# Four transformer blocks on one core: GpSimd takes part of the linear layer's products, z is read from PSUM, late score fills look for a free row group, and the build-time scheduler gets new issue times and a finer plan

## The chip, the core and the metric

The kernel runs on one core of a Trainium2 chip. The core has five engines that run their own instruction queues in order and wait for each other by semaphores: PE (TensorE, matmuls, with its weight loads shown apart as PEld), ACT (ScalarE), DVE (VectorE), POOL (GpSimd) and SP (SyncE, which only issues DMAs here). The metric is the device time of one execution in microseconds (us).

## What is computed

The input x has 2048 tokens of 512 values. Four blocks follow each other, each added to x after a layer norm: A, B, A, B, with the same weights in both A and both B.

```python
def _A_ref(x, wq, wk, wv, wo):            # 32 heads of 16, one K and V for all heads
    q = (x @ wq).reshape(B, S, H, Dh).transpose(0, 2, 1, 3)
    k, v = x @ wk, x @ wv
    p = softmax(einsum("bhqd,bkd->bhqk", q, k) * Dh ** -0.5)
    return einsum("bhqk,bkd->bhqd", p, v).transpose(0, 2, 1, 3).reshape(B, S, H * Dh) @ wo

def _B_ref(x, wqkv, wo):                  # linear attention, 32 heads of 16
    q, k, v = split(x @ wqkv)
    phi = lambda t: where(t > 0, t + 1, exp(t)) + 1e-6
    pq, pk = phi(q), phi(k)
    kv = einsum("bhsd,bhse->bhde", pk, v)
    z = einsum("bhsd->bhd", pk)
    num = einsum("bhqd,bhde->bhqe", pq, kv)
    den = einsum("bhqd,bhd->bhq", pq, z)[..., None] + 1e-6
    return (num / den).transpose(0, 2, 1, 3).reshape(B, S, D) @ wo

x = x + _A_ref(layernorm(x), ...)
x = x + _B_ref(layernorm(x), ...)
x = x + _A_ref(layernorm(x), ...)
x = x + _B_ref(layernorm(x), ...)
```

An A block and the B block after it are called a layer here, so there are two layers.

## The kernel before

**Who sets the order.** The order of the instructions isn't written out by hand. When the kernel is built, `Sched` runs a small model of the core: each operation is given to `add` with the engines that may do it, an estimated duration for each, what it reads and writes, a priority, and the buffers it takes and frees. Whenever an engine is free in the model, the ready operation with the smallest priority goes onto its queue. The result is five fixed queues, with semaphore waits where one operation needs another of a different engine (`finalize`, `emit`). So a change of the model's durations moves instructions on the chip. The model's knobs (priorities such as `PZ` and `PX`, limits such as `LEAD`, `DMIN` and `NPX`) are global names, and `PLAN` sets them anew at given model times, every 12 us.

**Attention (A).** The scores of one head, one key tile and 512 queries (in the first and last quarter: four heads of 128 queries) are a piece: 128 by 512, one bank of PSUM. There are 2048 pieces in a layer, 4096 in all. A piece's score matmul (L884) uses one row group of PE, 32 of the 128 rows, and up to four pieces on different row groups run beside each other. The exponentials are shared by two engines:

- ACT takes three banks or two at a time (`fill`): one exp (L1041) over 1536 or 1024 columns of PSUM into PTA.
- DVE takes single pieces from further on in the list, the late fills (`dstep`): L1098, called P1, makes an approximate exponential by integer arithmetic into PTD; three shifted copies of it are made for four pieces at once on DVE (L1169, called xo) or piece by piece on POOL (L1159, called xp), and the sum with four weighted copies of V corrects the approximation.

The products with V (L921, `pv`) add into bank 7 from both: one matmul for a piece of ACT, four for a piece of DVE. `norm` then copies the sums out (Eo, L933), transposes, divides and passes them on to the output projection, whose result is added to x (L1273).

**The B block.** While attention still runs, `b_prep` takes each finished token tile: layer norm, projections, and phi, which is an exp on ACT (L1281), a maximum on DVE (L1288, phr), a minimum on POOL (L1290, phm) and a sum on POOL (L1292, phs). `kv_block` sums k^T v and z over groups of tiles in PSUM; `kvm` (L1363) multiplies the result by a mask into kvacc or kvtmp, and kva (L1366) adds kvtmp to kvacc. At the last group zf (L1370) and kvf (L1372) add the two, zf is spread to zb (L1378), and den, the B block's denominators, can start.

From there each of the 16 token tiles goes through `b_tile`: den on PE; ln and exp(-ln) on ACT (L1409, L1410), which give 1/den; pqn on DVE (L1411), which multiplies pq by it; y2 on PE (num and output projection in one); and the residual (L1426 on DVE, or L1427 as a copy on DVE or ACT when PE has added x itself). After the first layer each tile goes straight into the second layer's layer norm (L692, L693, L695, L696, xn L711), its transposition (L723, xnT L729) and its K, V and Q (Kr L754/L755, Vaug L775, QT L808), so the layers overlap in a handover. After the second layer each tile is written out by a DMA.

**Rules of the model that matter here.** An operation with `port=True` on DVE isn't started while POOL works, and POOL isn't started while such an operation runs on DVE. A piecewise shift on POOL (`pair`) is made to wait for the DVE instruction before the last one planned, so that on the chip POOL doesn't run ahead of the plan. `idle` adds dummy matmuls where PE would be too quiet.

Of the kernel before, what the change touches and what calls it, by code (L numbers as in the profile page):

```python
# [11 lines left out]
ALU = mybir.AluOpType  # L12
# [8 lines left out]
LX = 0.338  # L21
# [32 lines left out]
PQL = 3.988  # L54
NPX = 6
# [5 lines left out]
SWITCH, PASS = 0.1, 0.217  # L61
PLAN = (
    (0.0, {'LX': 0.338, 'HOLD': 0.836, 'LEAD': 17, 'LEAD2': 14, 'NT0': 3, 'DMIN': 2, 'MP': 1, 'AP': 0.771, 'MF': 0.758, 'AF': 3.03, 'PCONT': 0.992, 'PX': 0.523, 'EVP': 1.5, 'EVX': 1.016, 'PQP': 3.044, 'PB': 1.6, 'PY': 4.497, 'PKV': 4.5, 'PTR': 1.57, 'PQL': 3.988, 'PHL': 3.959, 'PZ': 0.317, 'BK': 2.611, 'BKX': 0.376, 'BKR': 0.5, 'NPX': 6, 'PXP': 1.839, 'PXM': 0.451, 'PXA': 4.0}),
    (12.0, {'DMIN': 0, 'PX': 0.9, 'PXP': 2.685}),
    (24.0, {'LEAD': 16, 'DMIN': 1, 'AF': 2.905, 'PX': 0.523, 'PHL': 2.067, 'PZ': 0.131, 'PXP': 1.839, 'PXM': 0.53}),
    (36.0, {'LEAD2': 15, 'AF': 3.184, 'EVP': 1.614, 'PHL': 3.855, 'BKX': 0.07, 'PXM': 0.55}),
    (48.0, {'LEAD2': 14, 'AF': 2.533, 'PCONT': 0.746, 'PX': 1.328, 'EVP': 1.5, 'EVX': 1.127, 'PHL': 3.586, 'BKX': 0.376, 'NPX': 5}),
    (60.0, {'HOLD': 0.734, 'EVP': 0.64, 'PB': 3.033, 'PY': 3.776, 'PHL': 3.273, 'BKX': 0.628}),
    (72.0, {'AP': 0.2, 'PX': 2.292, 'PQP': 1.722, 'PB': 4.5, 'PXP': 1.517, 'PXM': 0.551}),
    (84.0, {'NT0': 5, 'PCONT': 0.778, 'EVX': 1.857}),  # L70
    (96.0, {'AF': 2.605, 'PHL': 1.421, 'BKR': 0.006}),
    (108.0, {'HOLD': 0.836, 'NT0': 3, 'AP': 0.771, 'AF': 2.905, 'PCONT': 0.78, 'PX': 3.908, 'EVP': 1.5, 'EVX': 1.016, 'PQP': 3.892, 'PB': 1.6, 'PY': 4.497, 'PQL': 2.469, 'PHL': 3.855, 'PZ': 0.906, 'BKX': 0.376, 'BKR': 0.5, 'NPX': 6, 'PXP': 1.839, 'PXM': 0.532}),
    (120.0, {'LX': 0.248}),
    (132.0, {'LX': 0.338, 'HOLD': 0.88}),
    (144.0, {'HOLD': 0.836, 'AP': 0.818, 'MF': 0.966, 'AF': 2.533, 'PCONT': 0.746, 'PX': 1.328, 'EVX': 1.127, 'PQP': 3.044, 'PQL': 3.988, 'PHL': 3.586, 'PZ': 0.131, 'NPX': 5, 'PXM': 0.55}),
    (156.0, {'AP': 0.771, 'MF': 0.758, 'AF': 2.905, 'PCONT': 0.992, 'PX': 3.679, 'EVX': 1.016, 'PY': 3.528, 'PQL': 3.445, 'PHL': 2.801, 'PZ': 1.146, 'BKR': 0.395, 'NPX': 6}),
    (168.0, {'HOLD': 0.57, 'NT0': 5, 'AP': 0.2, 'AF': 2.605, 'PCONT': 0.778, 'PX': 2.292, 'EVP': 0.64, 'EVX': 1.994, 'PQP': 1.6, 'PB': 4.5, 'PY': 3.776, 'PKV': 1.749, 'PQL': 3.988, 'PHL': 1.421, 'PZ': 0.131, 'BKX': 0.628, 'BKR': 0.006, 'NPX': 5, 'PXP': 1.517, 'PXM': 0.551}),
    (180.0, {'LEAD2': 24, 'PXM': 0.248}),
    (192.0, {'LX': 0.248, 'HOLD': 0.836, 'LEAD2': 14, 'NT0': 3, 'AP': 0.771, 'AF': 2.905, 'PCONT': 0.78, 'PX': 3.908, 'EVP': 1.5, 'EVX': 1.016, 'PQP': 3.892, 'PB': 1.6, 'PY': 4.497, 'PKV': 4.5, 'PQL': 2.469, 'PHL': 3.855, 'PZ': 0.906, 'BKX': 0.376, 'BKR': 0.5, 'NPX': 6, 'PXP': 3.89, 'PXM': 0.532}),
    (204.0, {'EVX': 2.046, 'PKV': 3.197, 'PXP': 4, 'PXM': 0.284}),  # L80
    (216.0, {'LX': 0.426, 'MF': 0.635, 'PQL': 1.0, 'BK': 2.24}),
    (228.0, {'HOLD': 0.674, 'EVX': 2.017, 'PB': 1.741, 'PKV': 3.92, 'PHL': 2.483, 'PXA': 3.668}),
    (240.0, {'HOLD': 0.655, 'BKR': 0.693}),
    (252.0, {'LX': 0.248, 'HOLD': 0.836, 'MF': 0.134, 'PX': 3.309, 'EVX': 2.046, 'PB': 1.6, 'PKV': 3.197, 'PQL': 2.469, 'PHL': 3.035, 'BK': 2.611, 'BKR': 0.637, 'PXA': 4.0}),
    (264.0, {'MF': 0.758, 'PX': 3.908, 'EVP': 2.13, 'PHL': 3.855, 'BKX': 1.267, 'BKR': 0.5, 'NPX': 5}),
    (276.0, {'DMIN': 2, 'EVP': 1.033}),
    (288.0, {'LX': 0.255, 'PX': 3.59, 'PTR': 1.67, 'BKR': 0.556}),
    (300.0, {'HOLD': 0.688, 'MP': 2, 'PQP': 2.339, 'PZ': 0.624, 'PXM': 0.374, 'PXA': 3.256}),
    (312.0, {'HOLD': 0.698, 'PX': 3.335, 'EVP': 1.382, 'PKV': 1.911, 'NPX': 6, 'PXM': 0.475}),
    (324.0, {}),  # L90
    (336.0, {'HOLD': 0.836, 'LEAD2': 16, 'MP': 1, 'PX': 2.368, 'EVP': 1.033, 'PQP': 3.892, 'PKV': 3.197, 'PZ': 0.906, 'BKX': 0.72, 'NPX': 5, 'PXM': 0.284, 'PXA': 4.0}),
    (348.0, {'LX': 0.338, 'HOLD': 0.743, 'LEAD2': 14, 'DMIN': 1, 'PCONT': 0.992, 'PX': 0.523, 'EVP': 1.5, 'EVX': 1.016, 'PQP': 4.5, 'PY': 4.236, 'PKV': 4.5, 'PTR': 1.57, 'PQL': 3.988, 'PZ': 0.131, 'BKX': 0.376, 'BKR': 0.5, 'NPX': 6, 'PXP': 1.839, 'PXM': 0.55}),
    (360.0, {}),
    (372.0, {'LX': 0.009, 'MF': 0.59, 'PY': 4.5}),
    (384.0, {'LX': 0.338, 'HOLD': 0.836, 'MF': 0.758, 'PCONT': 1.275, 'PX': 1.223, 'EVP': 0.567, 'PQP': 4.254, 'PY': 4.497, 'PZ': 0.225, 'PXA': 4.921}),
# [1396 lines left out]
```

## Time and profile before

| what | us |
|---|---|
| median of 3 runs | 1521.6 (1520.04 to 1524.15) |
| the profiled execution | 1516.72 |
| its span, first to last instruction | 1515.0 |
| mean granted TensorE clock | 0.997 of full speed |

| stage (by the trace) | from, to |
|---|---|
| ramp: loads, first layer norms, K, V, Q, first exps | 0 to some 42 us |
| attention of layer 1, with most of its B block's preparation | to some 720 |
| handover: last sums of B, its 16 tiles, start of layer 2 | to some 791 |
| attention of layer 2 | to some 1470 |
| end: last sums of B, its 16 tiles, output | to 1515 |

The costliest groups by line are the exps on ACT (L1041, 1187 of them, 1365.5 us busy), P1 on DVE (L1098, 1121, 744.5 us), the shifts on POOL (L1159, 1076, 659.2 us) and on DVE (L1169, 574, 392.0 us). PE's matmuls overlap, so its groups don't sum to its busy time. The 32 products pqn (L1411) on DVE have a mean of 682 ns. DMA moves 18 MB and is busy for a few per cent of the span.

A row of the profile's groups gives line, engine, operation, output and input, number, busy time, mean ns of one, and the engine's idle time just before them with what ended it. Records of an engine overlap a little at their ends, so a mean can be longer than the distance between two starts.

### The profile page before, as it was taken

The page shows a single profiled execution, that of the slowest core. Times are in us where ns is not written, and L with a number is a line of the kernel's source. Part 1 is how long each engine was busy: PE and PEld are TensorE (multiplying, and loading weights), DVE is VectorE, ACT ScalarE, POOL GpSimd, SP SyncE. Part 2 cuts the span into 40 slices and gives each one's busy share as a digit, 9 for nine tenths or more (in the row PEclk, how much of TensorE's full clock was granted, in tenths as well). Part 3 has the DMA queues.
Part 4 walks back from the last instruction along what each step waited for, and adds up shares of the span by engine and source line. Part 5 has one row for each costly group of instructions (what it writes and reads, how often), then busy time and mean ns, then how long its engine had stood idle before and what let it go on. Part 6 is the DMA issues. An engine that isn't in the chain of part 4 may idle for free.

```text
span 1515.0 us, 42368 instructions
## 1 busy us (share of the span) xinstructions
PE 1465.7 (97%) x18389; PEld 494.5 (33%) x18392; DVE 1373.7 (91%) x2419; ACT 1458.6 (96%) x1443; POOL 814.5 (54%) x1293
## 2 busy tenths in 40 slices
PE   6999999999999999999799999999999999999997
PEld 4333233322333222333453232332333232233334
DVE  6899998999988999899799999989998799989987
ACT  6999999999999999999699999999999999999986
POOL 2455666655574655565325645565555644465551
PEclk9999999999999999999999999999999999999999
DMA  4000000000000000000000000000000000000001
GB/s 142 2 8 8 5 9 8 4 4 4 16 8 5 5 5 16 9 9 8 3 3 4 6 9 5 12 6 5 5 5 15 5 5 5 5 19 9 5 9 59
DMA packets 46187, 17.98 MB, mean 12 GB/s; under 512 B 39856, under 2 KB 45488, under 8 KB 46000
## 3 DMA queue, kind: packets, MB, share of 16 engines
q1 hardware_dynamic: 46000, 15.27, 4.2%
q8 instruction: 144, 2.36, 0.6%
q14 instruction: 43, 0.35, 0.1%
HBM read 5.28 MB, written 2.10 MB: 5 GB/s over the span
## 4 chain that ended last, share of the span: by engine, by line
PE 48%; ACT 44%; DVE 7%; issue 1%; DMA 0%
ACT PTA L1041 41%; PE ps_all L921 19%; PE ps_all L884 19%; PE ps_all L632 9%; DVE PTD L1098 2%; PE ps_all L942 1%; DVE PTD L1169 1%; ACT e_buf L1281 1%; DVE stats L692 1%; DVE xn_buf L711 1%; DVE e_buf L1288 1%; DVE pqT L1411 0%; ACT e_buf L1409 0%; DVE Eo L933 0%; ACT e_buf L1410 0%
## 5 line engine op out<-in xcount | busy, mean ns | idle before, releaser
L1041 ACT ACTIVATE PTA<-ps_all 128x1536 bf16<-128x1536 f32 (+1 forms) x1187 | 1365.5, 1293 | 12.1 <-PE ps_all L884 8.8
L1159 POOL TENSOR_SCALAR PTD<-PTD 128x512 uint16<-128x512 uint16 x1076 | 659.2, 621 | 558.0 <-DVE PTD L1169 414.4
L1098 DVE TENSOR_SCALAR PTD<-ps_all 128x512 uint16<-128x512 f32 x1121 | 744.5, 683 | 76.0 <-PE ps_all L884 67.9
L884 PE MATMUL ps_all<-QT,Kr 32*128 32x512 bf16 x4147 | 654.2, 384 | 13.4 <-ACT PTA L1041 7.0
L921 PE MATMUL ps_all<-PTD,Vaug 128*32 128x512 bf16 x4484 | 614.1, 384 | 4.8 <-DVE Eo L933 3.4
L921 PE MATMUL ps_all<-PTA,Vaug 128*32 128x512 bf16 x2975 | 525.8, 386 | 0.0
L1169 DVE TENSOR_SCALAR PTD<-PTD 128x2048 uint16<-128x2048 uint16 x574 | 392.0, 702 | 1.7
L884 PEld LDWEIGHTS ps_all<-QT,Kr 32*128 32x128 bf16 x4147 | 161.3, 91 | 485.1 <-ACT PTA L1041 229.7
L921 PEld LDWEIGHTS ps_all<-PTD,Vaug 128*32 128x32 bf16 x4484 | 158.0, 94 | 204.8 <-issue 134.2
L921 PEld LDWEIGHTS ps_all<-PTA,Vaug 128*32 128x32 bf16 x2975 | 131.2, 94 | 167.6 <-issue 134.1
L632 PE MATMUL ps_all<-wqkv_sb,xnT 128*32 128x512 bf16 x1024 | 78.8, 396 | 3.0 <-ACT xnT L729 1.4
L1281 ACT ACTIVATE e_buf<-ps_all 128x512 f32<-128x512 f32 x64 | 40.2, 632 | 15.6 <-PE ps_all L632 10.9
L779 POOL TENSOR_SCALAR Vaug<-Vaug 128x32 bf16<-128x32 bf16 x48 | 15.2, 318 | 73.5 <-ACT Vaug L775 38.9
L1288 DVE TENSOR_SCALAR e_buf<-ps_all 128x512 f32<-128x512 f32 x60 | 40.9, 684 | 12.2 <-ACT e_buf L1281 11.8
L1290 POOL TENSOR_SCALAR e_buf<-e_buf 128x512 f32<-128x512 f32 x60 | 38.1, 637 | 23.1 <-ACT e_buf L1281 22.4
L632 PE MATMUL ps_all<-xnT,wq_sb 128*32 128x128 bf16 (+1 forms) x896 | 41.8, 298 | 3.6 <-issue 3.5
L692 DVE BATCH_NORM_STATS2 stats<-x_sb 128x6 f32<-128x512 bf16 x64 | 42.9, 678 | 1.2 <-DMA x_sb<-in_A_x_dram 1.0
L933 DVE COPY Eo<-ps_all 128x512 f32<-128x512 f32 x63 | 42.9, 681 | 1.1 <-PE ps_all L921 0.8
L632 PE MATMUL ps_all<-wo_sb,OT 128*32 128x512 bf16 x512 | 43.4, 382 | 0.0
L1292 POOL TENSOR_TENSOR pqT<-e_buf 128x512 bf16<-128x512 f32 x30 | 41.2, 1376 | 3.4 <-DVE e_buf L1288 2.9
L942 PE MATMUL ps_all<-identf,Eo 128*128 128x128 f32 x256 | 42.0, 287 | 0.2 <-DVE e_buf L1288 0.2
L1292 POOL TENSOR_TENSOR pk_tok<-e_buf 128x512 bf16<-128x512 f32 x30 | 39.4, 1312 | 0.8 <-DVE e_buf L1288 0.5
(88 smaller groups left out, 672.1 us busy)
## 6 DMA issues: line engine op xcount, KB each, us to landing
out_dram<-x_sb SPq DMA_DIRECT2D x16, 128.0 KB, 2.2
OT<-Osb SPq DMA_TRANSPOSE x120, 2.4
xnT<-xn_buf SPq DMA_TRANSPOSE x120, 2.4
wqkv_sb<-in_B_wqkv_dram SPq DMA_DIRECT2D x1, 1536.0 KB, 11.7
x_sb<-in_A_x_dram SPq DMA_DIRECT2D x3, 256.0 KB, 3.1
x_sb<-in_A_x_dram SPq DMA_DIRECT2D x1, 768.0 KB, 7.7
wq_sb<-in_A_wq_dram SPq DMA_DIRECT2D x1, 512.0 KB, 5.6
x_sb<-in_A_x_dram SPq DMA_DIRECT2D x1, 512.0 KB, 8.6
```

The source lines that it names most:

```text
L632: i = e.matmul(out[32 * c:32 * c + 32], lhsT=lhsT[:, 32 * c:32 * c + 32], rhs=rhs, start=start, stop=stop, skip_group_check=True)
L692: add(DV, tdv(512), lambda e: e.bn_stats(stats[:, t, 0:6], x_sb[:, t, :]), reads=[("x", t)], writes=[("st", t)], prio=prio, name="bn")
L884: x = e.matmul(bank(b0 + k), lhsT=Kr[r, m, kt * P:(kt + 1) * P], rhs=QT[r, self.units[u][0] % 2, gs, q0:q0 + n], start=True, stop=True)
L921: return e.matmul(ps[32 * c:32 * c + 32, 7 * 512:8 * 512], lhsT=Vaug[:, kt, r, :], rhs=src() if callable(src) else src, start=opened[0], s ...
L942: i = e.transpose(bank(ht.idx, P, qs * P), Eo[:, he.idx, qs * P:(qs + 1) * P], identf[:])
L1041: oe = add(AC, tac(m * 512), lambda e: e.activation(PTA[:, hp.idx, 0:m * 512], bank(SETS[s][0], m * 512), ACTF.Exp, scale=SCALE), deps=[o] ...
L1098: o = add(DV, tdv(512), lambda e: e.tensor_scalar(out=PTD[:, hp.idx, i * 512:(i + 1) * 512], in0=bank(db), scalar1=SCALE * LOG2E * 128.0, ...
L1159: return e.tensor_scalar(out=PTD[:, ht.idx, i * 512:(i + 1) * 512], in0=PTD[:, hp.idx, i * 512:(i + 1) * 512], scalar1=float(SHIFT[r]), sc ...
L1169: return e.tensor_scalar(out=PTD[:, ht.idx, 0:512 * m], in0=PTD[:, hp.idx, 0:512 * m], scalar1=float(SHIFT[r]), op0=ALU.add, **kw)
L1281: o1 = add(AC, tac(512), lambda e: e.activation(e_buf[:, he.idx, :], bank(h.idx), ACTF.Exp), deps=[o], uses=[h], acq=[he] if fast else [he ...
L1288: o2 = add(DV, tdv(512), lambda e: e.tensor_scalar(out=e_buf[:, hr.idx, :], in0=bank(h.idx), scalar1=0.0, scalar2=1e-6, op0=ALU.max, op1=A ...
L1292: add(PO, PHS, lambda e: e.tensor_tensor(out=dst, in0=sh(e_buf[:, hr.idx, :]), in1=sh(e_buf[:, he.idx, :]), op=ALU.add), deps=[o2, o3], us ...
```

## The change

Five things change in the scheduler and the operations, and with them the plan.

1. **Issue times in the model.** After issuing a score fill PE is taken up for 0.0045 us and 0.011 more for each further row group (before: 0.004). A shift on POOL costs 0.035 us less. A result of DVE counts as seen by POOL 0.05 us later. Any POOL operation longer than 0.4 us, not only the piecewise shifts, now waits for the last DVE instruction planned, or the one before it when DVE is at work in the model.
2. **Late fills.** `dstep` also avoids row groups on which a score matmul is still running in the model, when PE's last work was a score fill.
3. **Products on POOL.** pqn may go to DVE or POOL.
4. **z from PSUM.** zf adds kvacc and the PSUM columns of z themselves, before kvm, instead of kvacc and kvtmp after it.
5. **The plan** has a step every 4 us instead of 12, with new values; `BASE` holds what is set first. A new knob `NZ` adds a small fixed pseudo-random amount to priorities over 0.9, with the seed `SD`.

`activity` is written in a shorter way with the same values.

```diff
+JF = 1
+NZ = 0.0
+SD = 0
+PQE = 1
+ZD = 1
...
-    (12.0, {'DMIN': 0, 'PX': 0.9, 'PXP': 2.685}),
...
+    (1040.0, {'MF': 0.877, 'EVP': 2.53, 'PXM': 0.488}),
+    (1044.0, {}),
+    (1048.0, {'HOLD': 0.88, 'EVX': 0.959, 'PHL': 3.249, 'PXM': 0.595, 'PXA': 4.935, 'SD': 257}),
...
-PHM, PHS, POW, PXO, PXN = 0.62, 1.27, 0.92, (0.1, 1.1e-3), 0.62
+PHM, PHS, POW, PXO, PXN = 0.62, 1.27, 0.92, (0.035, 1.1e-3), 0.62
...
+        self.nadd += 1
+        if NZ and prio > 0.9:
+            o.prio += NZ * ((self.nadd * 40503 + SD * 9973) % 1009 / 1009.0 - 0.5)
...
-        return d.vis
+        return d.vis + (0.05 if d.eng == DV and o.engs[0] == PO else 0.0)
...
-        if e == PO and o.pair and len(self.order[DV]) > 1:
-            o.deps = o.deps + [self.order[DV][-2]]
+        if e == PO and (o.pair or o.dur[PO] > 0.4) and len(self.order[DV]) > 1:
+            o.deps = o.deps + [self.order[DV][-2 if self.tfree[DV] > self.now + 1e-9 else -1]]
...
-        self.tfree[e] = end if e != PE or o.pk[0] == "F" else self.now + 0.004
+        self.tfree[e] = end if e != PE or o.pk[0] == "F" else self.now + 0.0045 + (0.011 * (len(o.pk[1]) - 1) if o.pk[0] == "S" else 0.0)
...
-        def dstep(self, db, js):
+        def dstep(self, db, jset):
+            js = set(jset)
...
+            if sc.pk == "S" and JF:
+                js |= {j for j in range(4) if sc.pgrp.get(j, 0.0) > sc.now}
             good = [j for j in range(4) if j not in used and j not in js] or [j for j in range(4) if j not in js] or range(4)
...
-            js.add(self.pos[p][2])
+            jset.add(self.pos[p][2])
...
+            if final and ZD:
+                gs = slice(2 * hh, 2 * hh + 2)
+                add(DV, 0.07, lambda e, hh=hh, gs=gs, h=h: e.tensor_tensor(out=zf[:, gs], in0=kvacc[:, hh, 2 * P:KW], in1=bank(h.idx, 2, 2 * P), op=ALU.add),
+                    reads=[("kva", hh)], deps=[o], uses=[h], writes=[("zf", hh)], prio=PZ - 0.02, name="zf")
...
-                add(DV, 0.07, lambda e, hh=hh, gs=gs: e.tensor_tensor(out=zf[:, gs], in0=kvacc[:, hh, 2 * P:KW], in1=kvtmp[:, hh, 2 * P:KW], op=ALU.add),
-                    reads=[("kvt", hh), ("kva", hh)], writes=[("zf", hh)], prio=PZ - 0.02, name="zf", port=True)
...
-        o = add(DV, tdv(512), lambda e: e.tensor_tensor(out=pqT[:, :, ts], in0=pqT[:, :, ts], in1=e_buf[:, he.idx, :].rearrange("p (g n) -> p g n", g=NG), op=ALU.mult),
+        o = add((DV, PO) if PQE else DV, {DV: tdv(512), PO: PHS}, lambda e: e.tensor_tensor(out=pqT[:, :, ts], in0=pqT[:, :, ts], in1=e_buf[:, he.idx, :].rearrange("p (g n) -> p g n", g=NG), op=ALU.mult),
...
-    globals().update(PLAN[0][1])
+    globals().update(BASE)
```

Since the scheduler decides, the diff alone doesn't tell what moves. In the built programs these counts differ:

| engine, operation | before | after |
|---|---|---|
| ACT exps of three banks | 603 | 599 |
| ACT exps of two banks | 582 | 582 |
| ACT exps of one bank | 2 | 0 |
| ACT copies xnT, QT, Eo, steps zb | 13, 6, 1, 6 | 14, 7, 2, 8 |
| ACT copies Kr, Vaug, Msb | 11, 4, 4 | 7, 2, 3 |
| DVE P1 | 1121 | 1135 |
| DVE products pqn | 32 | 12 |
| POOL products pqn (13 in the handover, 7 at the end) | 0 | 20 |
| POOL piecewise shifts | 1076 | 1120 |
| DVE Kr, Vaug, Msb, xnT, zb | 21, 12, 4, 21, 2 | 25, 14, 5, 20, 0 |
| PE products with V: of PTA, of PTD | 2975, 4484 | 2961, 4540 |
| PE score matmuls | 4147 | 4135 |
| PE dummy matmuls (32 columns wide) | 140 | 112 |

At the end the built order now has the two sums kva before the last residual of attention; before, they stood between the last layer norm's statistics and its xn.

## The prediction

> **What bounds the kernel now.** I read the page's engine line first, then busy time by stage, the chain that ended last, and the single rows that the change touches.
>
> ```profile
> PE 1465.7 (97%) x18389; PEld 494.5 (33%) x18392; DVE 1373.7 (91%) x2419; ACT 1458.6 (96%) x1443; POOL 814.5 (54%) x1293
> ```
>
> Two engines look full. Matmuls are pipelined, so PE's 97% is not PE at its peak; the chain of waits has ACT's line L1041 (the exp) as its largest item, 41% of the span. The busy time in five stretches shows where ACT is full and where it is not (columns: length, then busy us of PE, weight loads, DVE, ACT, POOL; then the granted clock):
>
> ```profile
> 60.00:690.00 630.00, 619.72 (x6915) 195.53 (x6910) 585.36 (x997) 624.75 (x564) 373.72 (x581) 1.00 0.04 8
> 744.00:789.00 45.00, 40.98 (x1214) 25.25 (x1208) 41.76 (x102) 43.59 (x97) 7.38 (x22) 1.00 0.02 4
> 795.00:1450.00 655.00, 647.84 (x7177) 202.78 (x7173) 606.12 (x1040) 649.43 (x585) 360.31 (x562) 1.00 0.04 7
> 1478.00:1490.80 12.80, 7.53 (x221) 4.10 (x218) 8.83 (x20) 5.83 (x14) 5.54 (x6) 0.87 0.00 1
> 1490.80:1508.40 17.60, 16.44 (x455) 8.79 (x447) 16.69 (x28) 17.38 (x35) 0.00 (x0) 1.00 0.26 86
> ```
>
> In both attention stretches ACT is busy over 99% of the time and DVE 93%: there a microsecond of ACT work is a microsecond of the end. In the handover between the layers (744 to 789) ACT is at 97% and DVE at 93%, while POOL has 7 of 45 us: both are near their limit. In the short stretch before the last products (1478 to 1490.8) no engine is full; it is a serial chain. In the last 17.6 us ACT is full again (17.38), with DVE at 16.69 right behind it.
>
> **Prices.** Busy divided by count is too high where records overlap, so I take the distance between starts: 1.34 us for a three-bank exp alone, 2.275 for a pair of three and two banks (the chain has 53 exps in 60.31 us), thus 0.455 for one piece of 512. Other ACT steps by distance: 0.47 for a 512-wide copy, 0.37 for a Kr copy, 0.33 for a zb, 0.49 for the exp of L1281. On DVE: 0.60 for a 512-wide operation, 0.40 for Kr, 0.33 for xnT, 0.10 for Vaug.
>
> **Ramp, to the first exp of layer 1 with two banks.** The built order has ten three-bank exps there as before. From 22.3 to 40 us the chain of waits is mostly DVE. DVE loses three xnT copies and one Kr copy and gains two Vaug copies: -3 x 0.33 - 0.40 + 0.20 = -1.2 us. ACT gains 1.6 us of them, beside the 15 us in which it idles before 60 us. PE's 3.25 us stall at 14.2 us, for which the profile names no reason, I leave as it is. I count **-1.0**; bounds -3 and +1.5.
>
> **Attention.** Of the 4096 pieces ACT takes 2975 before and 2961 after. Eight of the 14 leave in the handover (35 to 27), six in the attention stages: -6 x 0.455 = -2.7. One more Eo copy on ACT: +0.6. DVE takes 14 more P1 (14 x 0.60) and has room: it is idle for some 90 us of these stretches. The free row group shortens waits for scores. In the table of waits:
>
> ```profile
> DVE PTD L1098 <- PE ps_all L884: 67.9, 158, 1.2
> ACT PTA L1041 <- PE ps_all L884: 8.8, 29, 0.7
> ```
>
> Only the second row is on ACT, and it bounds the gain at 8.8 us. A late fill goes to DVE, so what it gains is mostly the first row, which pays only as room for those 14 P1. No row shows which of ACT's waits are due to a late fill of the same row group: 0 to -8.8, nearer to 0; I take -0.9. Measured issue times and the finer plan add no instruction; their effect is the moves counted here. Together **-3.0**; bounds 0 and -10.
>
> **Handover.** Counted from layer 1's last two-bank exp to layer 2's first, ACT loses two three-bank exps (2.7), two of one bank (1.0), two xnT (0.9), five Kr (1.85), and one each of x_sb, Msb and L1281 (1.4), and gains a QT (0.5) and a zb (0.3): -7.1 us. DVE loses 13 of 16 products pqn (13 x 0.60 = 7.8) and a zb (0.2), and takes five Kr (2.0), two xnT (0.7), an x_sb (0.6) and an Msb (0.6): -4.1 us. DVE has 3.2 us of idle time in these 45, so it can give more than 4.1; ACT gives no more than 7.1, and PE, 91% busy in order, can't be pressed much further. Between -4.1 and -7.1 I take -5.0.
>
> The 13 products go to POOL. No row shows this operation there; the nearest are L1290 (one input, 0.637) and L1292 (two f32 inputs, median 1.273). With two inputs I take 1.27: 16.5 us for 13, in a queue that works 7 us here. Behind them wait the copies of Vaug (24, 8.0 us busy), which the first products with V need; POOL idles 45.5 us before them now, so that cover holds. Seven products in a row take 8.9 us; before, nine tiles took 11.2 us, so POOL's pace does not hold back PE.
>
> **The rule against it.** DVE and POOL get in each other's way:
>
> ```profile
> L1366 DVE TENSOR_TENSOR kvacc<-kvacc,kvtmp x12: 393/428/1490, 478.0 to 1480.5; 128x258 f32<-128x258 f32 x12
> L711 DVE TENSOR_SCALAR xn_buf<-x_sb,mv,rstd x64: 320/404/1468, 6.2 to 1481.9; 128x512 bf16<-128x512 bf16 x64
> ```
>
> (Shortest, median, longest ns.) The two sums at 1480.14 show the case: the second starts 0.2 us after an L1292 on POOL, and the pair takes 1.80 us; the longest L1366 is 1.06 us over the median. [...] By the row the mean of L711 lies only 44 ns over its median, though POOL is over half busy in attention, because the planner keeps such pairs apart (port=True). 16 xn in the handover at twice that excess, POOL's products being twice as long as its shifts, are 1.4 us; DVE isn't always the last, so I take +0.8 for the handover, bounds 0 and +10.
>
> z from PSUM: zf follows the matmul directly, no longer behind two kvm, so 0.76 us leaves the chain, and a read of two PSUM columns may cost slightly more than 0.15: -0.7. Handover: -5.0 + 0.8 - 0.7 = **-4.9**.
>
> **End.** The chain there reads
>
> ```profile
> 1480.14 0.09 DVE mv L693
> 1480.22 1.72 DVE kvacc L1366 x2
> 1481.94 0.63 DVE xn_buf L711
> ...
> 1488.08 0.76 DVE kvtmp L1363 x2
> 1488.84 0.08 DVE zf L1370
> 1488.92 0.02 issue
> 1488.94 0.99 ACT zb L1378 x3
> ```
>
> The plan now sets the two kvacc sums before the last residual, so xn can start when rstd is there: ACT's second step ends near 1480.7, hence -1.2, not -1.7. z gives -0.7. Seven of 16 products leave DVE, -4.2 us, but here ACT is the bound: two steps for each of 16 tiles, already back to back from 1490.8 to 1508.3, and ACT gets a zb (0.33) and an x_sb copy (0.47) more before its last step. So the products earn almost nothing at the end: -1.2 - 0.7 + 0.8 = **-1.1**; bounds -3 and +1.
>
> **Waits added on POOL.** Every POOL operation longer than 0.4 us now waits for the DVE instruction planned beside it: of the 60 minima L1290 39 wait for DVE after the change, none before. Behind one stand the shifts L1159 (PE waits 12.6 us for them in all, off the chain) and L1292, which frees e_buf for ACT's L1281 (4.4 us). Cover: POOL idles 46% of the span. 0; at worst +2.
>
> **Sum.** -1.0 - 3.0 - 4.9 - 1.1 = -10.0 us on a span of 1515.0, so 1505.0; the profiled execution took 1516.7, so 1506.7. The runs have a median of 1521.6, 4.9 above the profiled execution; I keep that distance: **1511.6**.
>
> **Rivals.** (B) ACT's idle time shrinks too. It sums to 56 us: 15 before 60 us, 14 from 720 to 795, 17 after 1465, and some 11 in attention. If a quarter of the first three goes as well, that is another -11: 1500.6. For it: plan steps three times as fine. Against: these are chains of single steps, and most keep their links. (C) The saving hides: ACT's freed time in the handover is spent waiting for PE, whose order there is fixed, and the ramp stays. Only -3.0 of attention is left, less if waits return: 1518.6. For it: PE at 91% in these 45 us. Against: by the distance between their starts its matmuls fill some 41 of the 53 us from 742 to 795. (D) Slower: the lock. Each product holds DVE as long as the longest L1366 was held, 20 x 1.06 = 21 us, less the 10.0: 1532. It decides from about 14 to 15 full blocks of 20, where the gain is gone with 0.3% more. Against: DVE keeps only 3 products in the handover. (E) The change not doing what it says is excluded in part: the order does have 20 products on POOL and zf on PSUM.
>
> **How the numbers follow.** Likeliest case 0.72 (own range 1506 to 1517), B 0.15, C 0.09, D 0.04. 0.3% is 4.6 us, about what a measurement of this kernel can tell from no change. Faster: the likeliest, B and a little of C, 0.88; within: 0.08; slower: 0.04. The range takes half of B and of C: 1502 to 1518.6.
>
> **What would show it.** ACT busy near 1452 with its idle time at 50 to 54; in the handover ACT still over 95%, L1411 partly on POOL at about 1.27 us; L711 with a longest near 1.5 us but a mean below 0.5; no kvacc between L693 and xn at the end, zb right behind zf. I am wrong if ACT falls below 95% in the handover (C), if L711's or pqn's mean rises by half a microsecond there (D), or if the end shortens by far more than 1.1 us.

## The result, and the profile after

| | before | after |
|---|---|---|
| median of 4 runs, us | 1521.7 (1520.04 to 1524.15) | 1502.37 (1501.01 to 1503.33) |
| the profiled execution, us | 1516.72 | 1501.46 |
| its span, us | 1515.0 | 1499.3 |

The change makes the kernel faster by 19.3 us: the ratio is 0.9871, with an interval from 0.9854 to 0.9888. Measured again later beside 19 executions of the kernel before (experiment 11), the ratio is 0.9884, or 16.4 us; the two intervals overlap. The forecast was 1511.6, so the sign and about half of the size were right, and the time measured lies 0.4 us inside the low end of the stated range of 1502 to 1518.6.

In all fences below, lines of the new code stand where others stood before: the score matmul is L1139 (was L884), the exp on ACT L1296 (L1041), P1 L1356 (L1098), the shift on DVE L1427 (L1169) and on POOL L1417 (L1159), xn L966 (L711), kva L1632 (L1366), the sum phs on POOL L1554 (L1292), pqn L1678 (L1411), PE's projections L887 (L632). Fences of b_wait and b_warm, which are kernels with the old code, keep the old lines. First the page's engine line of the kernel after:

```profile
PE 1458.0 (97%) x18393; PEld 500.0 (33%) x18393; DVE 1363.4 (91%) x2413; ACT 1452.0 (97%) x1435; POOL 850.4 (57%) x1357
```

ACT's busy time is 1452.0, as forecast. The span minus it, ACT's idle time, went from 56.4 to 47.3 us, where 50 to 54 were forecast. The busy time in five stretches that answer to those shown of before (length, then PE, weight loads, DVE, ACT, POOL, then the granted clock):

```profile
60.00:690.00 630.00, 623.15 (x6967) 200.91 (x6964) 592.20 (x1019) 624.65 (x562) 370.99 (x588) 1.00 0.04 8
736.00:781.00 45.00, 41.05 (x1198) 24.31 (x1194) 38.63 (x98) 39.77 (x88) 22.07 (x37) 1.00 0.02 4
787.00:1440.00 653.00, 645.72 (x7220) 207.36 (x7220) 611.43 (x1051) 650.26 (x586) 384.40 (x610) 1.00 0.04 8
1462.30:1475.00 12.70, 8.09 (x237) 4.54 (x233) 7.56 (x19) 6.43 (x15) 6.83 (x7) 1.00 0.00 1
1475.00:1492.60 17.60, 16.80 (x468) 9.05 (x458) 13.39 (x20) 17.60 (x36) 8.06 (x7) 1.00 0.23 76
```

In the handover (second row) ACT is busy for 88% only, where it was 97%. It was the forecast's own sign for being wrong there. In the last row ACT has no gap at all, and DVE, which gave seven products to POOL, has 4.2 us to spare: what it gave up there earns little (0.5 us by experiment 4). The waits of the kernel after, in the same two rows as before (total us, times, longest):

```profile
DVE PTD L1356 <- PE ps_all L1139: 60.2, 125, 1.3
ACT PTA L1296 <- PE ps_all L1139: 5.9, 20, 0.7
```

Both are shorter (67.9 and 8.8 before). And the instructions that POOL had held up (shortest, median, longest ns). The row of the shift before was:

```profile
L1169 DVE TENSOR_SCALAR PTD<-PTD x574: 411/685/1760, 44.5 to 1467.0; 128x2048 uint16<-128x2048 uint16 x190, 128x1024 uint16<-128x1024 uint16 x1, 128x1536 uint16<-128x1536 uint16 x1
```

After the change:

```profile
L966 DVE TENSOR_SCALAR xn_buf<-x_sb,mv,rstd x64: 320/405/433, 6.2 to 1468.0; 128x512 bf16<-128x512 bf16 x64
...
L1632 DVE TENSOR_TENSOR kvacc<-kvacc,kvtmp x12: 416/430/609, 456.1 to 1459.0; 128x258 f32<-128x258 f32 x12
...
L1427 DVE TENSOR_SCALAR PTD<-PTD x572: 542/704/1387, 41.0 to 1448.5; 128x2048 uint16<-128x2048 uint16 x190, 128x1536 uint16<-128x1536 uint16 x1
```

The longest xn was 1468 ns before and is 433, the longest kva 1490 and is 609, the longest shift 1760 and is 1387. Counting DVE instructions more than 0.35 us over the median of their group gives 11 before, 9.9 us over in all, and 4 after, 2.2 us over. This is what the forecast had not seen coming: more work on POOL, and less blocking.

By stage the span of the profiled executions changed as follows. A serial stretch reaches from the end of attention's last exp to the first zb; b_wait is experiment 2 below, the kernel before with the new waits on POOL alone.

| stage, us | before | b_wait | after |
|---|---|---|---|
| ramp, to the first two-bank exp | 40.4 | 40.5 | 39.0 |
| attention of both layers, to each last exp | 1364.4 | 1360.5 | 1356.9 |
| serial stretch of layer 1 | 18.8 | 16.4 | 16.0 |
| from zb to layer 2's first two-bank exp | 47.6 | 47.8 | 48.0 |
| serial stretch of layer 2 | 17.7 | 16.6 | 13.2 |
| from zb to the end | 26.1 | 26.2 | 26.2 |
| span | 1515.0 | 1508.0 | 1499.3 |

The chain of waits of the kernel after in the last serial stretch (start us, us, what):

```profile
1465.43 0.70 DVE x_sb L1535
...
1467.44 0.10 DVE mv L948
1467.54 0.02 issue
1467.56 0.21 ACT veps L950
...
1468.04 0.42 DVE xn_buf L966
...
1469.58 1.08 PE ps_all L887 x16
...
1472.92 0.17 DVE zf L1627
1473.09 0.02 issue
1473.11 0.42 ACT zb L1645 x2
```

From mv to xn it is 0.60 us (1.80 before), since no kva stands there any more; zf comes right behind the projections' and kv's matmuls.

### The profile page after: what moved, and what is told of

The parts are those of the page before. It is cut to its first block, busy times and chain, and to the rows that moved or that the text cites. A ratio compares the mean times of both kernels' runs of the same rounds, so it can differ in the third digit from the quotient of the medians.

```text
span 1499.3 us, 42503 instructions
## 1 busy us (share of the span) xinstructions
PE 1458.0 (97%) x18393; PEld 500.0 (33%) x18393; DVE 1363.4 (91%) x2413; ACT 1452.0 (97%) x1435; POOL 850.4 (57%) x1357
## 4 chain that ended last, share of the span: by engine, by line
PE 60%; ACT 24%; DVE 15%; issue 1%; POOL 0%; DMA 0%
PE ps_all L1176 24%; PE ps_all L1139 23%; ACT PTA L1296 22%; PE ps_all L887 10%; DVE PTD L1356 8%; DVE PTD L1427 4%; PE ps_all L1197 2%; DVE Eo L1188 1%; ACT e_buf L1543 1%; DVE stats L947 1%; DVE e_buf L1550 0%; PE ps_all L978 0%; DVE x_sb L1535 0%; ACT xnT L984 0%; DMA x_sb<-in_A_x_dram 0%
## 5 line engine op out<-in xcount | busy, mean ns | idle before, releaser
L1296 ACT ACTIVATE PTA<-ps_all 128x1536 bf16<-128x1536 f32 (+1 forms) x1181 | 1361.1, 1294 | 9.2 <-PE ps_all L1139 5.9
L1417 POOL TENSOR_SCALAR PTD<-PTD 128x512 uint16<-128x512 uint16 x1120 | 681.1, 618 | 483.6 <-DVE PTD L1427 354.6
L1356 DVE TENSOR_SCALAR PTD<-ps_all 128x512 uint16<-128x512 f32 x1135 | 747.3, 681 | 64.8 <-PE ps_all L1139 60.2
L1139 PE MATMUL ps_all<-QT,Kr 32*128 32x512 bf16 x4135 | 650.3, 384 | 8.0 <-ACT PTA L1296 3.7
L1427 DVE TENSOR_SCALAR PTD<-PTD 128x2048 uint16<-128x2048 uint16 (+1 forms) x572 | 399.3, 710 | 2.2
L1139 PEld LDWEIGHTS ps_all<-QT,Kr 32*128 32x128 bf16 x4135 | 169.8, 91 | 484.4 <-ACT PTA L1296 213.3
L887 PE MATMUL ps_all<-wqkv_sb,xnT 128*32 128x512 bf16 x1024 | 77.0, 388 | 0.9 <-ACT xnT L984 0.7
L887 PE MATMUL ps_all<-xnT,wq_sb 128*32 128x128 bf16 (+1 forms) x896 | 44.2, 298 | 4.8 <-issue 4.6
L1554 POOL TENSOR_TENSOR pk_tok<-e_buf 128x512 bf16<-128x512 f32 x30 | 38.1, 1271 | 10.2 <-DVE PTD L1427 8.1
L1554 POOL TENSOR_TENSOR pqT<-e_buf 128x512 bf16<-128x512 f32 x30 | 38.1, 1272 | 7.8 <-DVE PTD L1427 4.6
L887 PE MATMUL ps_all<-wo_sb,OT 128*32 128x512 bf16 x512 | 41.2, 382 | 0.9 <-ACT OT L1520 0.8
L1678 POOL TENSOR_TENSOR pqT<-pqT,e_buf 128x512 bf16<-128x512 bf16 x20 | 23.2, 1168 | 29.7 <-ACT e_buf L1677 23.1
```

What stands on the lines that cost most here:

```text
L887: i = e.matmul(out[32 * c:32 * c + 32], lhsT=lhsT[:, 32 * c:32 * c + 32], rhs=rhs, start=start, stop=stop, skip_group_check=True)
L1139: x = e.matmul(bank(b0 + k), lhsT=Kr[r, m, kt * P:(kt + 1) * P], rhs=QT[r, self.units[u][0] % 2, gs, q0:q0 + n], start=True, stop=True)
L1296: oe = add(AC, tac(m * 512), lambda e: e.activation(PTA[:, hp.idx, 0:m * 512], bank(SETS[s][0], m * 512), ACTF.Exp, scale=SCALE), deps=[o] ...
L1356: o = add(DV, tdv(512), lambda e: e.tensor_scalar(out=PTD[:, hp.idx, i * 512:(i + 1) * 512], in0=bank(db), scalar1=SCALE * LOG2E * 128.0, ...
L1417: return e.tensor_scalar(out=PTD[:, ht.idx, i * 512:(i + 1) * 512], in0=PTD[:, hp.idx, i * 512:(i + 1) * 512], scalar1=float(SHIFT[r]), sc ...
L1427: return e.tensor_scalar(out=PTD[:, ht.idx, 0:512 * m], in0=PTD[:, hp.idx, 0:512 * m], scalar1=float(SHIFT[r]), op0=ALU.add, **kw)
```

## The experiments

Twelve kernels ran. Where a kernel keeps the order of another, only the named instructions differ; "made anew" means that the scheduler made another order. Each was timed beside the kernel before; that median was 1519.2 to 1519.7 in the three sessions. The kernel after had 1502.37 when it was first measured and 1502.87 in the third session, so differences to it of less than some 1 us mean nothing. An edit that moves instructions is followed by lines that sort the list again by its dependencies; they are left out below ("...").

**1. The new waits on POOL taken away.** The rule of the waits alone is the old one again:

```diff
-        if e == PO and (o.pair or o.dur[PO] > 0.4) and len(self.order[DV]) > 1:
-            o.deps = o.deps + [self.order[DV][-2 if self.tfree[DV] > self.now + 1e-9 else -1]]
+        if e == PO and o.pair and len(self.order[DV]) > 1:
+            o.deps = o.deps + [self.order[DV][-2]]
```

> The kernel after, with one thing undone: only the piecewise shifts on POOL wait for a DVE instruction again, and for the one before the last planned. The order on every engine is that of the kernel after. [...] Rival (the waits neither cost nor earn, as the prediction priced them): 1502.4 within 1.5 us. Second rival (the waits cost something): below 1501.

Measured: 1512.09 (1511.90 to 1513.92), ratio to before 0.9953 [0.9939, 0.9967]: 9.7 us above the kernel after. Both rivals are out, also the first, on which the forecast stood: the waits earn. Of the long cases of before, the shift (1758 ns) and kva (1482 ns) come back; xn does not (695 ns). Since the order is the same, instructions can be compared one by one, and nearly all of the loss comes at six places. This is the timeline of one of them (start us, us, engine, line; in brackets how long the engine idled before, and for whom):

```profile
860.34 2.41 DVE L1427 TENSOR_SCALAR PTD<-PTD 128x2048 uint16<-128x2048 uint16 x2
860.49 1.71 POOL L1554 TENSOR_TENSOR pk_tok<-e_buf 128x512 bf16<-128x512 f32 x1
...
862.67 0.68 DVE L1356 TENSOR_SCALAR PTD<-ps_all 128x512 uint16<-128x512 f32 x1
...
863.40 0.98 PE L1139 MATMUL ps_all<-QT,Kr 32*128 32x512 bf16 x5 [0.83 <-DVE PTD L1356]
...
864.05 1.45 ACT L1296 ACTIVATE PTA<-ps_all 128x1536 bf16<-128x1536 f32 x1 [0.44 <-PE ps_all L1139]
...
864.60 1.03 PE L1176 MATMUL ps_all<-PTD,Vaug 128*32 128x512 bf16 x5 [0.21 <-DVE Eo L1188]
```

The sum on POOL starts while the first of two shifts is under way. It takes 1.71 us instead of 1.27, and the second shift, which begins at 860.99, takes 1.758 us instead of 0.70. PE then waits 0.83 us for P1, and ACT 0.44 us for scores. The same place in the kernel after:

```profile
856.40 1.33 DVE L1427 TENSOR_SCALAR PTD<-PTD 128x2048 uint16<-128x2048 uint16 x2
...
857.65 0.68 DVE L1356 TENSOR_SCALAR PTD<-ps_all 128x512 uint16<-128x512 f32 x1
...
857.81 1.27 POOL L1554 TENSOR_TENSOR pk_tok<-e_buf 128x512 bf16<-128x512 f32 x1 [1.23 <-DVE PTD L1427]
```

The sum waits 1.23 us for the shifts, which costs nobody anything, and then runs beside a P1, which takes its usual 0.68 us: of the 63 P1 that overlap a sum or product on POOL in this profile none takes over 0.70 us. The sums and products over 1.15 us on POOL that start while a DVE shift is under way are 10 in the kernel before, none after, 16 here. So what matters is which DVE instruction the long one meets: the sum takes 1.71 us when it starts beside the shift, and 1.27 us beside P1.

A second cost follows at the same place. Three windows of 3.4 us of this kernel (columns as in the stretches above; the clock is the number behind POOL's, here 1.00 and 0.50):

```profile
857.60:861.00 3.40, 3.40 (x44) 1.06 (x36) 2.83 (x6) 3.40 (x5) 2.77 (x5) 1.00 0.00 0
861.00:864.40 3.40, 2.56 (x22) 0.53 (x21) 3.40 (x5) 2.96 (x4) 1.57 (x2) 1.00 0.00 0
864.45:867.80 3.35, 3.20 (x27) 0.65 (x27) 2.58 (x5) 2.07 (x2) 2.15 (x5) 0.50 0.00 0
```

After a window with 22 matmuls instead of 44, PE has half its clock for 3.41 us. ACT's exps end up 1.5 us later after the place near 157 us, where the clock stays at 1.00, and 2.5 us later after each of the two places (861 and 905) behind which it halves.

**2. The new waits alone, in the kernel before.** The same two lines, put into the old code, whose order stays:

```diff
-        if e == PO and o.pair and len(self.order[DV]) > 1:
-            o.deps = o.deps + [self.order[DV][-2]]
+        if e == PO and (o.pair or o.dur[PO] > 0.4) and len(self.order[DV]) > 1:
+            o.deps = o.deps + [self.order[DV][-2 if self.tfree[DV] > self.now + 1e-9 else -1]]
```

> The kernel before with one thing of the change alone: every POOL operation over 0.4 us waits for the DVE instruction planned beside it. The order on every engine is that of the kernel before. Theory, formed after the kernel after without these waits took 1512.1: a DVE shift, xn or kva of the kernel before is held up to 1.07 us by a long POOL sum that starts beside it (11 cases, 9.9 us over the medians, in its trace), and some of the holds leave PE so quiet that its clock halves for 3.41 us; with the waits the cases fall to 4 or fewer, no POOL sum starts beside a shift, and the time falls by 6 to 11 us to 1509 to 1514. Rival (the waits pay only in the new order, which was planned with them): within 2 us of the kernel before.

Measured: 1510.32 (1509.74 to 1512.40) against 1519.19, ratio 0.9936 [0.9921, 0.9952]; 8.9 us faster. The theory holds. The longest shift of this kernel:

```profile
L1169 DVE TENSOR_SCALAR PTD<-PTD x574: 412/685/1343, 44.7 to 1461.0; 128x2048 uint16<-128x2048 uint16 x190, 128x1024 uint16<-128x1024 uint16 x1, 128x1536 uint16<-128x1536 uint16 x1
```

Two held cases are left of 11. So the one edit in two lines makes about half of the whole gain, with none of the moves that the forecast counted. Part of it seems to come by way of the clock: the median of the mean granted clock is 0.9975 in its six executions and 0.996 in those of the kernel before beside it.

**3. The new waits at the long operations only.**

```diff
-        if e == PO and (o.pair or o.dur[PO] > 0.4) and len(self.order[DV]) > 1:
-            o.deps = o.deps + [self.order[DV][-2 if self.tfree[DV] > self.now + 1e-9 else -1]]
+        if e == PO and (o.pair or o.dur[PO] > 1.0) and len(self.order[DV]) > 1:
+            o.deps = o.deps + [self.order[DV][-2 if o.dur[PO] <= 1.0 or self.tfree[DV] > self.now + 1e-9 else -1]]
```

> The kernel after in its own order, but the new waits stand only at POOL's operations over 1.0 us (60 sums and 20 products); the minima have none and the 1120 piecewise shifts have the old rule. Theory (one long sum beside a DVE shift is the costly case): nearly the whole gain stays, 1502 to 1504.5. Rival (the waits pay by keeping the 1120 shifts and the minima on the plan): 1507 to 1512, as without the new waits.

Measured: 1502.86 (1501.87 to 1504.54), ratio 0.9886 [0.9866, 0.9905]. All of the gain stays: the new waits at 80 long operations of POOL's 1357 instructions carry it.

**4. All 20 products back on DVE,** in the order of the kernel after:

```diff
+    for o in al:
+        if o.name == "pqn" and o.eng == PO:
+            o.eng = DV
...
```

> The kernel after in its own order, but all 20 products pqn of POOL are made by DVE, at the same places in the order. Theory of the prediction: DVE gets 13 x 0.60 = 7.8 us more in the handover, where it and ACT are both near full, so the handover gets 2 to 4 us longer, and the 7 at the end (4.2 us of DVE) cost 0 to 1 us because ACT is the bound there: 1504.5 to 1507.5. Rival (the handover between zb and layer 2's first two-bank exp gained nothing from this part, since PE and the links between the engines set it): 1502.4 within 1 us, or below it, since a product is seen 0.4 us sooner on DVE (0.73 against 1.17 us).

Measured: 1505.48 (1504.27 to 1506.89), ratio 0.9908 [0.9894, 0.9922]; 3.1 us above the kernel after, inside the theory's range. From zb to the first two-bank exp of layer 2 it takes 51.9 us instead of 48.0, from the last zb to the end 0.5 us more. The busy time in that stretch of the handover is, for this kernel,

```profile
734.00:785.90 51.90, 43.09 (x1318) 25.45 (x1318) 47.86 (x118) 42.66 (x96) 7.05 (x23) 1.00 0.02 4
```

for the kernel after,

```profile
732.50:780.50 48.00, 43.04 (x1318) 26.02 (x1318) 41.06 (x105) 42.66 (x95) 21.66 (x35) 1.00 0.02 4
```

and for the kernel before with the new waits alone (b_wait):

```profile
735.30:783.20 47.90, 43.34 (x1329) 27.00 (x1329) 44.14 (x110) 46.41 (x104) 7.31 (x21) 1.00 0.02 4
```

In this order POOL's share is needed. But DVE 3.1 us and ACT 3.8 us less busy, the last two rows, bring no shorter stretch: 48.0 and 47.9. PE is busy for some 43 of 48 us in both. The chain of waits of the kernel after runs mostly over PE from 747 to 772 us, with two gaps of 1.24 and 0.51 us:

```profile
747.37 3.33 PE ps_all L887 x220
750.70 1.24 issue
751.94 2.06 PE ps_all L887 x82
...
756.63 2.50 PE ps_all L887 x109
759.13 0.51 issue
759.64 1.59 PE ps_all L887 x42
...
767.85 1.72 PE ps_all L887 x61
```

In b_wait the chain stands on PE from 746.8 to 763.7 us and then in part on ACT:

```profile
746.77 7.03 PE ps_all L632 x279
...
764.46 1.45 ACT PTA L1041
```

That PE's order sets the 48 us is read from these two chains; no edit here tests it by itself.

**5. Two moves of the serial chain undone.** zf behind both kvm in both layers, and the end's two kva between mv and xn again (in the order of the kernel after):

```diff
+    kv_ = [o for o in al if o.name == "kva"][-2:]
...
+    rs_ = max(i for i, o in enumerate(al) if o.name == "xn")
+    al[rs_:rs_] = kv_
+    zfs = [o for o in al if o.name == "zf"]
...
+        k1 = al.index(at) + 1
+        al[k1:k1] = mv_
...
```

The edit also takes away POOL's waits on these two kva (among the lines left out).

> The kernel after in its own order, with two moves of the chain undone: zf is planned behind both kvm in both layers (it still reads PSUM), and the two last sums kva of the end are put back between the last layer norm's statistics and its xn. Theory (the serial stretches carry their steps one to one to the end): +0.7 us in the handover, +0.7 us for zf and +0.7 to 1.2 us for kva at the end, together 1504.5 to 1505.0; the stretch from the last exp to the first zb at the end goes from 13.2 back to some 15 us, and from 16.0 to 16.7 in the handover. Rival (these steps are hidden beside another wait, such as PE's): 1502.4 within 0.8 us.

Measured: 1507.46 (1506.59 to 1507.93), ratio 0.9918 [0.9903, 0.9934]; 5.1 us above the kernel after, twice what was expected. The end's serial stretch has 15.7 us (some 15 were expected), the handover's 17.1 (16.7), but at the end the clock halves twice, and what follows zb gets longer too: 49.1 us instead of 48.0 in the handover and 27.7 instead of 26.2 at the end. One of the two kva, no longer waited for by POOL, is held (826 ns, median 441). So the two moves' own time isn't measured alone here.

**6. zf alone late,** the second half of that edit:

```diff
+    zfs = [o for o in al if o.name == "zf"]
...
+        k1 = al.index(at) + 1
+        al[k1:k1] = mv_
...
```

> The kernel after in its own order with zf alone planned behind both kvm in both layers. Putting back zf and the two kva together cost 5 us in the median, 2.2 were expected, and the granted clock fell to half twice at the end instead of never. Theory (the moved steps cost only their own time, and the rest is the half clock that the longer pause of PE brings): zf alone costs 0.7 us in each serial stretch, the end's pause of PE stays near 1.8 us with no half clock there, and the time is 1 to 2 us above the kernel after. Rival (zf is the costlier of the two moves): 3 us or more above.

Measured: 1507.16 (1504.68 to 1508.73), ratio 0.9914 [0.9898, 0.9930], against 1502.87 of the kernel after beside it: 4.3 us, and the rival is nearer. The chain at the end says what it is made of:

```profile
1474.09 4.64 PE ps_all L887 x101
1478.73 0.02 issue
1478.75 0.76 DVE kvtmp L1629 x2
1479.51 0.07 DVE zf L1627
```

kvm before zf is 0.76 us, as forecast. But PE's part is 4.64 us where the kernel after has 3.3 (1469.58 to 1472.89): the clock halved at 1473.89. Up to there the end has the instructions of the kernel after in the same order, where the same pause of PE (1.83 us there) brought no half clock; why it did here isn't shown. Of the 4.7 us between the two profiled spans (1506.5 against 1501.8 of the kernel after beside it), 2.0 are the end's serial stretch (15.15 against 13.16), 0.7 what follows it, 1.7 the handover's serial stretch and 1.5 the ramp, in which this execution has a second half-clock window, while attention is 1.2 us shorter; so one profile can't say how much of it belongs to zf.

**7. PE kept busy in the kernel after's handover:** 8 more groups of dummy matmuls before the last transposition.

```diff
+    for z_, n_ in ((zi_[2], 0), (zi_[0], 8)):
+        d_ = max(i for i in range(z_) if al[i].name == "dummy" and al[i].pk[0] == "P")
+        al[d_ + 1:d_ + 1] = [copy.copy(al[d_]) for _ in range(n_)]
...
```

> The kernel after in its own order, with 8 more groups of dummy matmuls (32 matmuls, nothing computed) in the serial stretch of layer 1's handover, before the transposition of the last xn. In the kernel after PE idles 2.1 us there and the granted clock drops to 0.50 for 3.41 us; at the end it idles 1.8 us and doesn't drop. Theory (the drop lengthens the projections and the kv sums, and shortens when PE is kept busy): the clock stays at 1.00 near 727 us, proj to kv gets 0.5 to 1.0 us shorter, the time is 1501.4 to 1501.9. Rival (PE isn't the link there, or the handover absorbs it afterwards): 1502.4 within 0.3 us.

Measured: 1502.30 (1501.97 to 1502.87), ratio 0.9886 [0.9871, 0.9902]. The clock stays at 1.00, the serial stretch is 0.8 us shorter (15.2), and the tiles behind it take 0.6 us longer (48.6): the rival's second half, the handover takes it back. Why it does is open. In experiment 3's profiled execution, which has no such matmuls, the clock happened to stay at 1.00 there too, and both parts are short (15.2 and 47.8 us).

**8. The same in both serial stretches of the kernel before,** 14 groups each:

```diff
+    for z_, n_ in ((zi_[2], 14), (zi_[0], 14)):
+        d_ = max(i for i in range(z_) if al[i].name == "dummy" and al[i].pk[0] == "P")
+        al[d_ + 1:d_ + 1] = [copy.copy(al[d_]) for _ in range(n_)]
...
```

> The kernel before in its own order with 14 more groups of dummy matmuls (56 matmuls, nothing computed) in each of the two serial stretches, where PE stood still 3.46 us and the granted clock then was 0.50 for 3.41 us. Theory (a half clock costs about 1 us where PE is a link): the clock stays at 1.00 in both stretches and the time falls by 1.5 to 2.5 us. Rival (the handover takes it back, as it did when the kernel after got such dummies): only the end's share of about 1 us, or nothing.

Measured: 1518.12 (1514.36 to 1521.59) against 1519.24, ratio 0.9989 [0.9976, 1.0001]: unclear. Both stretches have the full clock and are 1.4 and 1.0 us shorter, as the theory has it, but the executions scatter by 7 us, and their mean granted clock with them: 1514.36 and 1514.48 at 1.000, 1519.74 to 1521.59 at 0.994. In the profiled one (0.995) half-clock windows appear elsewhere: there are three in a row in attention:

```profile
163.60:173.80 10.20, 10.20 (x68) 2.25 (x68) 6.74 (x13) 6.17 (x7) 3.11 (x6) 0.50 0.05 10
```

They follow a held shift (1758 ns at 159.12), and attention of layer 1 takes 3.9 us more than in the kernel before's profile (685.7 against 681.8).

**9. The old plan in the new code** (`PLAN` and its first values are those of before; order made anew):

```diff
-    (4.0, {'HOLD': 0.885, 'LEAD': 15, 'PHL': 3.727, 'PXM': 0.436}),
...
+    (12.0, {'DMIN': 0, 'PX': 0.9, 'PXP': 2.685}),
```

> The new code with the plan of the kernel before, so that the scheduler makes another order. Theory (the waits give some 10 us, and products on POOL and z from PSUM give a few more, whatever the plan): 1504 to 1510, with few or no held shifts. Rival (the new plan is what earns, and the new rules need it): 1513 or more.

Measured: 1556.62 (1552.86 to 1558.39), ratio 1.0227 [1.0206, 1.0249]. The theory is out. The number falls on the rival's open side, but 54 us above the kernel after it is worse than either kernel; the next run shows that it can't be read as the rival meant.

**10. A yardstick for orders made anew:**

```diff
+        if 'HOLD' in c_:
+            c_ = dict(c_, HOLD=c_['HOLD'] + 0.002)
```

> The kernel after with 0.002 added to the knob HOLD wherever the plan sets it, so that the scheduler makes another order by the same rules. It is a yardstick: how far the time moves when an order is made anew by values that nobody has tried on the chip. If such orders lie close together, 1501 to 1505. If the plan's 261 steps were fitted to one order, 1506 to 1514. Few or no held shifts in both cases.

Measured: 1549.64 (1548.93 to 1550.71), ratio 1.0193 [1.0173, 1.0212], 47 us above the kernel after and far outside both guesses. Its waits on ACT:

```profile
ACT PTA L1296 <- PE ps_all L1139: 41.3, 52, 6.0
```

With ACT as busy as before (1458.0 us), it waits 41 us for scores, up to 6.0 at a time, where the kernel after waits 5.9 in all (the kernel of experiment 9 waits 36.9). Only four DVE instructions are held. So the plan's values fit one order, and the two orders made anew here cost 47 and 54 us. That takes the meaning from experiment 9, and it is why the row-group rule of the late fills was not tried by itself: it changes the order. The old code with the new plan was not tried either. What the issue times, the late fills and the finer plan earn apart from each other is therefore not shown.

**11. The kernel after again,** and **12. two more things for it:** the two long sums that still hold a shift wait for it, and the dummies of experiment 7.

```diff
+    xo_ = [o for o in al if o.name == "xo" and o.eng == DV]
+    ps_ = [o for o in al if o.name == "phs"]
+    for a_, b_ in ((6, 104), (37, 385)):
+        ps_[a_].deps = ps_[a_].deps + [xo_[b_]]
...
```

> The kernel after, unchanged, on the same chip as the three runs beside it, so that differences of 1 to 2 us can be read. Same chip as its other runs or not, 1500 to 1503.5.

> The kernel after in its own order with two things added: the two long sums on POOL that still hold a DVE shift (0.63 and 0.68 us over the median, at 283 and 1002 us) wait for that shift, and layer 1's handover gets 8 more groups of dummy matmuls (nothing computed). Theory (a held shift costs its time and at times a half clock besides): 1 to 2 us below the kernel after beside it. Rival (in these two places other waits take the time): the same within 0.7 us.

Measured: 1502.87 (1500.55 to 1503.93), ratio 0.9884 [0.9864, 0.9903], and 1501.52 (1500.92 to 1502.84), ratio 0.9881 [0.9865, 0.9897]. The two holds are gone (longest shift 1144 ns), and between 21 and 1500 us the profile has no half clock. A gain of 1.4 us in the medians, with intervals that overlap: it can't be told from none.

## Why the prediction was right and wrong

- **The step that failed: "Cover: POOL idles 46% of the span. 0; at worst +2".** The waits on POOL were priced by what they delay. They pay by what they keep apart: -8.9 us when added alone (experiment 2), +9.7 when taken away (experiment 1). The trace of before held the evidence: 11 held DVE instructions, 9.9 us over their medians. The forecast quoted two of the rows, kva's and xn's, but not the shift's, which has 6 of the 11. It read them as a risk that grows with POOL's new products (+0.8, rival D) and didn't ask whether the new waits would remove them. What rival D starts from does occur (the longest kva is 1490 ns before, its median 428), but the change works against it: 11 cases became 4.
- **Attention, -3.0.** The forecast's attention ends at layer 1's last two-bank exp; by this edge it fell by 5.1 us. The waits alone make 3.9 of it, and 1.2 are left for what the forecast counted. (By the table's edge, the last exp of any size, the same numbers are 7.4, 3.9 and 3.6.)
- **Handover, -4.9.** By the forecast's own edges, layer 1's last two-bank exp to layer 2's first, it fell from 68.75 to 64.00, which looks like a hit. But b_wait already has 66.5, so the moves earn 2.5. The term "Between -4.1 and -7.1 I take -5.0" was too large. What was priced rightly lies at the front: after the last two-bank exp there stood a three-bank and a one-bank exp that aren't there any more, and with them 2.3 us are gone. Behind zb both engines lost work as counted (DVE 3.1, ACT 3.8 us from b_wait to after), and the stretch didn't shorten: 47.8 and 48.0, with PE busy for 43 us of it. The forecast had named this as rival C and set it aside by a density of matmul starts (41 of 53 us). Experiment 4 shows that the products' move isn't worthless: with them on DVE this order is 3.9 us longer there.
- **The lock, +0.8,** came out at nothing: no product on POOL starts beside a shift, and none of the handover's 13 holds a DVE instruction; at the end one DVE product takes 1.12 us instead of 0.69 beside one on POOL. A product on POOL takes 1.17 us (1.27 was taken).
- **z from PSUM, -0.7** per layer: 0.76 us of kvm have left the chain, as worked out. What that is worth in the time isn't shown, since experiment 6 disturbed the clock as well.
- **End, -1.1:** it fell by 4.4 us, 3.4 of them beyond b_wait. Of the sum's terms -1.2 (kva) and -0.7 (z) hold in the chain, +0.8 for ACT's two added steps came out at 0.2 (26.1 to 26.2 us). What was missing: the last residual of attention comes 1.4 us sooner after the last exp (5.5 us instead of 6.9; before, the sums of k^T v of the group before stood just ahead of it on PE), and the half clock that before had after a pause of 3.46 us isn't there, so that from the last projections to kv it takes 2.93 us instead of 3.99. The pause before and after:

```profile
1482.62 0.40 PE L723 MATMUL ps_all<-ident,xn_buf 128*128 128x128 bf16 x4 [3.46 <-DVE xn_buf L711]
```

```profile
1468.51 0.40 PE L978 MATMUL ps_all<-ident,xn_buf 128*128 128x128 bf16 x4 [1.83 <-DVE xn_buf L966]
```

- **Ramp, -1.0:** -1.4 in the pair of profiles, though the ramp of the kernel after has 38.7 to 41.3 us in profiles of kernels with the same ramp, so this can't be told.
- **"I keep that distance" of 4.9 us** between the median and the profiled execution: after, it is 0.9. 19 executions of the kernel before in one session say what it is made of: the seven with a mean granted clock of 0.997 to 0.998 have a median of 1517.35, the seven with 0.991 to 0.992 one of 1521.9. A half-clock window takes 3.41 x 0.5 / 1517 = 0.0011 of the mean clock, so 0.005 are 4 to 5 windows, and by this estimate each costs about 1 us. The profiled execution of before was one with few. The kernel after has 0.997 or 0.998 in all of its first four.
- **Rival B, 1500.6,** came nearest in number, and its first half is so: ACT's idle time fell by 9.1 us, where B had 11. But 5.8 of it came with the waits alone (50.7 us idle in b_wait), not from the finer plan that B gave as its reason.

So a term of about -9, the waits, stood at zero. The moves, priced at -10.0, earned 8.7 us in the profiles from b_wait to after and some 7.5 in the medians. That this comes near is in part luck: attention and the handover were priced at twice what they earned or more, the end at a third, and the errors offset each other.

## What to carry to other kernels

A wait added to an engine with slack is priced not only by what it delays but by what it then runs beside: look for the instructions whose longest case is far over their median, and ask whether the wait moves the partner away. An engine's idle share in a stage pays only if no other engine in order stands right behind it; compare the busy time of all of them before counting a move. And where a tuned schedule is fitted to one order, try an edit in the frozen order, since an order made anew moved the time here by 47 us for a knob changed by 0.002.

## What was not expected of the hardware

- The half clock came after quite different stretches of PE. In the profiles of before and after each half-clock window lasts 3.41 us. In the 3.41 us ahead of those that come after the ramp PE was busy for 0.49 us (8 matmuls, before, from 732.02 us), for 0.32 (4, before, from 1479.53) and for 1.29 (25, after, from 723.66); in experiment 1 for 2.56 of 3.40 us (22, the second of the three rows there), with a pause of 0.83 us. But the clock stayed at 1.00 after 3.4 us from 1466.1 us of the kernel after, in which PE was busy for 1.19 us (17 matmuls) and paused for 1.83. So neither the count nor the pause alone tells here when the clock halves.
- Half the clock can last longer: 10.2 us in a row in experiment 8 (the row at 163.6 us there).
- A POOL sum that comes second also takes longer (1.71 us instead of 1.27 in experiment 1; 1.58 to 1.77 us for the ten that start beside a shift in the kernel before), and the DVE shift queued next takes 1.758 us instead of 0.70 and ends 0.55 us after the sum: one bad start delays both.
